# The last stage of a linear-attention and spectral-mixing kernel: the fifth chunks of two batches in one half-wide unit, and more of the adds of x on GpSimd

## The chip, the cores and the metric

One Trainium2 chip; the kernel runs on one of its cores. The metric is the device time in microseconds (us) of one execution. A program's time here is the median of several executions; the profile shows one execution, and its own time stands beside its span below. TensorE is called PE, VectorE DVE, ScalarE ACT, GpSimd POOL and SyncE SP. "SPq" and "ACTq" in the profile are the sequencers of SP and ACT, which issue DMAs.

## The reference

```python
def phi(x):                                   # q, k: (8, 8, 576, 64); w_phi: (64, 128)
    proj = np.einsum('bhsd,df->bhsf', x, w_phi)
    proj = proj - np.max(np.abs(proj), axis=-1, keepdims=True)
    return np.concatenate([np.exp(proj), np.exp(-proj)], axis=-1)
q_p, k_p = phi(q), phi(k)
kv = np.einsum('bhsf,bhsd->bhfd', k_p, v)
z = np.sum(k_p, axis=2)
num = np.einsum('bhsf,bhfd->bhsd', q_p, kv)
den = np.einsum('bhsf,bhf->bhs', q_p, z)[..., None] + 1e-06
x = (num / den).transpose(0, 2, 1, 3).reshape(8, 576, 512)
X = np.fft.rfft(x, axis=1)                    # the first 64 modes are mixed, the others dropped
Yr = einsum('bmd,mde->bme', Xr, w_r) - einsum('bmd,mde->bme', Xi, w_i)
Yi = einsum('bmd,mde->bme', Xr, w_i) + einsum('bmd,mde->bme', Xi, w_r)
y = np.fft.irfft(Y, n=576, axis=1)
u = x + y
out = u + np.maximum(u @ w_ch, 0.0)           # (8, 576, 512) float32
```

## The kernel before

The work has three stages. The first (lines 491 to 583) computes the attention for 32 steps of a batch and two heads (or two batches and one head), and writes x into `xs_all`; the Fourier transform and the first products with `w_r` and `w_i` run in between. The second (lines 661 to 683) waits for the last weights to be loaded, ends the mixing of modes, and computes two products ahead: `xw`, which is x times `w_ch`, and for each batch the spectrum Y (`yall`) and Y times `w_ch` (`zall`), both in bf16. The third (lines 686 to 749) is where the change lies. It computes, for each batch and each chunk of rows,

- relu(x w_ch + irfft(Y w_ch)): in `chan`, PE adds `xw` (through an identity matrix, L689) and `CI` times `zall` (L691) in PSUM, and ACT writes the relu into the output tile (L693);
- x + irfft(Y): in `spec`, PE puts `CI` times `yall` into PSUM (L702), DVE adds it to the output tile (L705), and x is added either by PE, as one more matmul with the identity ahead of L702 (L700), or, in a unit that is called "late", by POOL on the output tile after DVE (L710).

The 576 rows of a batch lie on the partitions in two halves of 288: partition p of the lower half (0 to 63) holds the rows 9p to 9p + 4 as the chunks 0 to 4, and partition 64 + p the rows 9p + 5 to 9p + 8 as the chunks 0 to 3. So the fifth chunk (number 4) of a batch fills the lower 64 partitions alone; its upper half is computed and not used.

A unit of work is two chunks, a PSUM tile of 128 x 2 x 512 floats for each of `chan` and `spec`. There are 20 units, here numbered u0 to u19. For each pair of batches b and b + 4 (b = 0 to 2) there are four wide units (chunks 0 and 1 of batch b, chunks 2 and 3 of it, then the same for batch b + 4), followed by one unit with the fifth chunks of both: u0 to u3 and u4, u5 to u8 and u9, u10 to u13 and u14. The last pair starts with its fifth chunks: u15, and then u16 to u19. Late are, for b up to 2, the first wide unit of each batch and the unit of fifth chunks; in the last pair u15 and u16: 11 of the 20 units.

All of it stands in an order that is written out by hand (`manual_schedule`): each engine takes its instructions in program order. Step n issues `chan` and `spec` of unit n, then on SP the output DMA of the lower half of the partitions, and then on ACT the DMA of the upper half for an earlier unit:

```python
        LAG = 3
        copies.pop(0)()
        for n in range(len(units) + LAG):
            if copies:
                copies.pop(0)()
            if n < len(units):
                u = units[n]
                u["tags"] = ("T2", "T3") if n % 2 == 0 or n < 3 else ("T0", "T1")
                chan(u)
                spec(u)
                for dst, src in u["dmas"][0:1]:
                    nc.sync.dma_start(dst, src)
            for lag, late in ((2, False), (3, True)):
```

An output DMA of a batch carries its chunks 0 to 3 (512 KB for each half of the partitions) and is attached to the second wide unit; in the last pair each wide unit has its own two DMAs of 256 KB. The fifth chunks of two batches leave in one DMA of 256 KB on SP, from the lower half of the partitions (`o4[0:64]`, in the tile `Yacc`). The two PSUM pairs (T2, T3 and T0, T1) alternate: `chan` of unit n waits for the relu of unit n - 2, and `spec` of unit n for DVE's add of unit n - 2. At the start four copies of the last quarter of `zall` (ACT, L656) and `yall` (DVE, L657) stand between the first units.

## Time and profile before

| what | value |
|---|---|
| time of the program | 465.15 us, median of 3 runs (464.51 to 466.84) |
| the profiled execution's own time | 468.21 us |
| its span in the profile | 466.4 us (1.8 us lie around it) |
| the third stage: first matmul of `chan`, last matmul of `spec` | 423.94 us, 456.14 us |
| DVE's last add | 456.75 to 457.97 us |
| first and last issue of an output DMA | 430.48 us, 460.78 us |
| last byte written | about 465.2 us |
| HBM written (the output) | 9.44 MB |

The profile cuts the span into 40 slices of 11.66 us; a digit is an engine's busy share of a slice in tenths, so the third stage is the last four digits of each row. The timeline gives start and duration of each instruction, with the tile that is written, the shapes, and in brackets how long the engine had been idle and who released it. A matmul's row lasts 0.38 us because the array is a pipeline; successive matmuls of 512 columns start 0.216 us apart. "128*64" in a matmul's row means 128 rows and 64 columns of the array in use. q1 is the DMA queue of SP, q10 that of ACT, q0 that of POOL.

### The profile page before, as it was taken

The numbers are of one execution on the slowest core, as the hardware profiler recorded it, in microseconds if no ns is written. First come the engines' busy times: TensorE is split into PE (matmuls) and PEld (weight loads), VectorE is DVE, ScalarE is ACT, GpSimd is POOL, SyncE is SP. The second block draws the span as 40 slices with busy tenths as digits, with TensorE's granted clock in tenths as the row PEclk, the third lists the DMA queues.
The fourth block names the chain that finished last, engine by engine and source line by source line (L and its number), as shares of the span: only waits on it lengthen the run. The fifth ranks groups of instructions, "written<-read, shape, count | busy, mean of one in ns | idle before, by whom it ended". The sixth has DMA issues, their size and how long they took to land.

```text
span 466.4 us, 11013 instructions
## 1 busy us (share of the span) xinstructions
PE 305.9 (66%) x4602; PEld 201.7 (43%) x4615; DVE 301.0 (65%) x414; ACT 254.9 (55%) x516; POOL 199.8 (43%) x253
## 2 busy tenths in 40 slices
PE   2665886735765777657374645566688887867991
PEld 1454664623543645435243433345344444433440
DVE  6688799854988788876455554755322637446882
ACT  3865786743686868765455454555123524516671
POOL 4695477545563346643343333333111221001781
PEclk9997599895899669996777786886799999989997
DMA  8999999999999999999999999999999999930997
GB/s 184 250 249 242 236 216 217 229 206 217 220 228 218 229 218 224 218 229 218 218 214 223 207 229 208 206 207 208 207 207 207 207 207 207 207 65 1 234 317 260
DMA packets 83553, 99.08 MB, mean 212 GB/s; under 512 B 3248, under 2 KB 75568, under 8 KB 82736
## 3 DMA queue, kind: packets, MB, share of 16 engines
q0 software_dynamic: 73872, 74.72, 96.2%
q1 hardware_dynamic: 8672, 19.40, 14.1%
q10 hardware_dynamic: 960, 4.26, 2.9%
q8 instruction: 36, 0.59, 0.5%
q14 instruction: 13, 0.11, 0.1%
HBM read 163.64 MB, written 9.44 MB: 371 GB/s over the span
## 4 chain that ended last, share of the span: by engine, by line
DMA 33%; DVE 21%; issue 20%; PE 13%; ACT 5%; POOL 5%; SPq 1%; DVEq 0%; ACTq 0%; POOLq 0%
DMA wi<-in_moe_w_i_dram 18%; DMA wr<-in_moe_w_r_dram 7%; DVE mkq L222 6%; DMA q<-in_q_dram 4%; DVE xs_all L325 4%; DVE nd L311 3%; DVE tB L304 3%; ACT AA L229 3%; POOL vaug L259 2%; PE psB L689 2%; PE psA L702 2%; PE psB L691 2%; DMA vn<-in_v_dram 2%; DMA qn<-in_q_dram 1%; ACT e L251 1%
## 5 line engine op out<-in xcount | busy, mean ns | idle before, releaser
L259 POOL TENSOR_TENSOR vaug<-vn,ee 128x576 bf16<-128x576 f32 x64 | 72.6, 1152 | 59.6 <-ACT ee L244 50.6
L229 ACT ACTIVATE AA<-psT 128x1024 bf16<-128x1024 f32 x64 | 62.0, 1021 | 47.3 <-PE psT L197 46.8
L151 POOL DMA_DIRECT2D wr<-in_moe_w_r_dram x24 | 21.9, 913 | 113.3 <-PE psY L389 107.6
L251 ACT ACTIVATE e<-mkq 64x4 f32<-64x4 f32 (+1 forms) x128 | 26.3, 206 | 65.8 <-DVE mkq L222 61.4
L233 ACT ACTIVATE AA<-psk 128x1024 bf16<-128x1024 f32 x64 | 61.3, 1009 | 0.0
L624 ACT CAST xw<-psW 128x1024 bf16<-128x1024 f32 x20 | 20.2, 1012 | 54.3 <-PE psW L622 52.3
L389 PE MATMUL psY<-wi,XT 128*32 128x512 bf16 x192 | 25.2, 470 | 34.7 <-DMA wi<-in_moe_w_i_dram 34.7
L389 PEld LDWEIGHTS <-XT 128*32 128x32 bf16 x384 | 18.0, 167 | 64.2 <-issue 53.9
L622 PE MATMUL psW<-wchb,sT 128*128 128x512 bf16 x150 | 38.3, 389 | 3.6 <-ACT xw L624 2.7
L222 DVE TENSOR_REDUCE mkq<-psk 128x8 f32<-128x1024 f32 x32 | 38.8, 1211 | 0.7 <-PE psk L188 0.7
L408 DVE TENSOR_TENSOR Yacc<-psY,Yacc 128x512 f32<-128x512 f32 x16 | 11.0, 689 | 43.5 <-PE psY L389 43.4
L222 DVE TENSOR_REDUCE mkq<-psq 128x8 f32<-128x1024 f32 x32 | 38.9, 1216 | 0.2 <-PE psq L188 0.2
L389 PE MATMUL psY<-wr,XT 128*32 128x512 bf16 x192 | 24.7, 468 | 19.6 <-DMA wr<-in_moe_w_r_dram 8.3
L275 PE MATMUL kvz<-vaug,AA 64*128 64x65 bf16 x1152 | 30.0, 212 | 7.9 <-POOL vaug L264 6.2
L179 DVE COPY kT<-ptr 128x640 bf16<-128x640 bf16 x32 | 15.7, 492 | 29.5 <-PE ptr L173 29.5
L304 DVE TENSOR_TENSOR tB<-psNB,e 128x650 f32<-128x650 f32 x32 | 26.6, 832 | 11.0 <-PE psNB L294 10.3
L294 PEld LDWEIGHTS <-AA 128*128 128x128 bf16 x640 | 29.2, 110 | 10.2 <-issue 8.5
L325 DVE TENSOR_TENSOR xs_all<-nd,rden 128x640 bf16<-128x640 f32 x32 | 31.9, 998 | 1.1
L710 POOL TENSOR_TENSOR of<-of,xs_all 128x1024 f32<-128x1024 f32 x7 | 14.9, 2129 | 38.7 <-DVE of L705 38.5
L275 PEld LDWEIGHTS <-AA 64*128 64x128 bf16 x1152 | 25.7, 108 | 12.1 <-issue 7.9
L197 PE MATMUL psT<-qT,w 64*128 64x512 bf16 x64 | 15.8, 485 | 21.7 <-DVE mkq L222 21.6
L311 DVE TENSOR_TENSOR nd<-psNA,tB 128x650 f32<-128x650 f32 x32 | 26.7, 835 | 3.8 <-DVE tB L304 0.5
(120 smaller groups left out, 713.0 us busy)
## 6 DMA issues: line engine op xcount, KB each, us to landing
wr<-in_moe_w_r_dram POOLq DMA_DIRECT2D x24, 1024.0 KB, 23.8
wi<-in_moe_w_i_dram POOLq DMA_DIRECT2D x24, 1024.0 KB, 28.0
wr<-in_moe_w_r_dram POOLq DMA_DIRECT2D x16, 512.0 KB, 18.6
wi<-in_moe_w_i_dram POOLq DMA_DIRECT2D x16, 512.0 KB, 21.0
vn<-in_v_dram SPq DMA_DIRECT2D x24, 288.0 KB, 5.7
q<-in_q_dram POOLq DMA_DIRECT2D x12, 288.0 KB, 19.9
k<-in_k_dram POOLq DMA_DIRECT2D x12, 288.0 KB, 21.4
out_dram<-of SPq DMA_DIRECT2D x6, 512.0 KB, 6.1
```

What stands on the lines that cost most here:

```text
L222: nc.vector.tensor_reduce(out=o, in_=i, axis=AX.X, op=ALU.max, apply_absolute_value=True)
L229: nc.scalar.activation(AA[:, 0, ab, 0:1024].rearrange("f (x j p) -> f j x p", j=2, p=64), st["psT"].rearrange("f j (x p) -> f j x p", p=64 ...
L233: nc.scalar.activation(AA[:, 1, ab, 0:1024].rearrange("p (c j f) -> p j c f", c=4, j=2), st["psk"], ACT.Exp, scale=sc)
L251: nc.scalar.activation(e2[64 * jj:64 * jj + 64, hh, 0:NCH - jj], mkq[64 * hh:64 * hh + 64, 1, 5 * jj:5 + 4 * jj], ACT.Exp, scale=2.0)
L259: nc.gpsimd.tensor_tensor(out=vaug[:, ab, :, 0:64], in0=st["v"], in1=ee[:, ab, :].unsqueeze(2).to_broadcast([128, 9, D_]), op=ALU.mult,)
L275: nc.tensor.matmul(kvz[:, hh, ab * 65:(ab + 1) * 65], lhsT=AA[r, 1, ab, 128 * j:128 * j + 128], rhs=vaug[r, ab, j, :], start=(j == 0), sto ...
L294: nc.tensor.matmul(p[:, hh, 65 * c:65 * c + 65], lhsT=AA[:, 0, ab, x:x + 128], rhs=kvzF[:, hh, ab * 65:(ab + 1) * 65], start=True, stop=True,)
L304: nc.vector.tensor_tensor(out=tB, in0=st["psNB"], in1=e2.unsqueeze(3).to_broadcast([128, 2, NCH, 65]), op=ALU.mult,)
L311: nc.vector.tensor_tensor(out=nd, in0=st["psNA"], in1=st["tB"], op=ALU.add)
L325: nc.vector.tensor_tensor(out=xo, in0=nd[:, :, :, 0:64], in1=rden.to_broadcast([128, 2, NCH, 64]), op=ALU.mult,)
L389: nc.tensor.matmul(psY[32 * j:32 * j + 32, :], lhsT=XT[:, c0:c0 + 32, m], rhs=wt[ri][:, 2 * j + par, :], start=(par == 0 and ri == 0), sto ...
L622: nc.tensor.matmul(ps[:, x, :], lhsT=sT[:, x, dc, :], rhs=wchb[:, dc, :], start=(dc == 0), stop=(dc == 3))
```

## The change

The fifth chunks of two batches become one chunk: batch b in the partitions 0 to 63, batch b + 4 in 64 to 127. Each of the four units u4, u9, u14, u15 has eight matmuls with 64 columns of weights in place of six with 128, a relu and a DVE add of 512 elements per partition in place of 1024, no POOL add (x comes through PE), and two DMAs of 128 KB, the lower half on SP and the upper on ACT, in place of one of 256 KB. Of the wide units, ten in place of seven are late: for b up to 2 all but the last (u0 to u2, u5 to u7, u10 to u12), and in the last pair u16 as before. So six wide units in place of nine get x through PE. A wide unit's matmuls stand in another order in `spec` (identity for both chunks, then `CI` for both). ACT issues the upper half's DMA of a late unit four steps after it, in place of three; since the DMA of a batch b hangs on its second wide unit, which is late now, it moves from step n + 2 to n + 4, behind that of batch b + 4 in ACT's order (a loop over the lag of 2 comes first). `LAG` is 4.

```diff
+    def parts(u):
+        if "half" not in u:
+            for x, (b, c) in enumerate(u["bc"]):
+                yield slice(0, 128), x, b, c, slice(0, 128)
+        else:
+            for x, (b, c) in enumerate(u["bc"]):
+                yield slice(64 * x, 64 * x + 64), 0, b, c, slice(0, 64)
+
     def chan(u):
         ps = psum.tile([128, 2, DMODEL], F32, name="psB", tag=u["tags"][0])
...
+        todo = list(parts(u))
+        both = [lambda r, x, b, c, m: nc.tensor.matmul(
+                    ps[r, x, :], lhsT=ident_b[:, m], rhs=xw[:, b * NCH + c, :],
+                    start=True, stop=False),
+                lambda r, x, b, c, m: nc.tensor.matmul(
+                    ps[r, x, :], lhsT=CI[:, c, m], rhs=zall[:, b, :], start=False, stop=True)]
+        if "half" in u:
+            for f in both:
+                for a in todo:
+                    f(*a)
+            nc.scalar.activation(u["o"], ps[:, 0, :], ACT.Relu)
...
     def spec(u):
         ps = psum.tile([128, 2, DMODEL], F32, name="psA", tag=u["tags"][1])
...
+        late = u["late"]
+        todo = list(parts(u))
+        if not late:
+            for r, x, b, c, m in todo:
+                nc.tensor.matmul(ps[r, x, :], lhsT=ident_b[:, m], rhs=xs_all[:, b * NCH + c, :],
+                                 start=True, stop=False)
+        for r, x, b, c, m in todo:
+            nc.tensor.matmul(ps[r, x, :], lhsT=CI[:, c, m], rhs=yall[:, b, :],
+                             start=late, stop=True)
+        o = u["o"]
+        nc.vector.tensor_tensor(out=o, in0=ps[:, 0, :] if "half" in u else ps, in1=o, op=ALU.add)
+        if late:
+            b, c = u["bc"][0]
             i = b * NCH + c
...
+            nc.gpsimd.tensor_tensor(out=o, in0=o, in1=xs_all[:, i:i + 2, :], op=ALU.add)
...
-        o4 = Yacc[:, 2 * b:2 * b + 2, :]
+        o4 = Yacc[:, 2 * b, :]
...
-                               late=c == 0 and not (last and x == 1), dmas=dmas))
-        u4 = dict(bc=((b, 4), (b + 4, 4)), o=o4, late=True,
-                  dmas=[(out[b::4].rearrange("x (p n) e -> p x n e", n=9)[:, :, 4, :], o4[0:64])])
+                               late=(x, c) == (0, 0) if last else (x, c) != (1, 2), dmas=dmas))
+        u4 = dict(bc=((b, 4), (b + 4, 4)), o=o4, late=False, half=True,
+                  dmas=[(out[b + 4 * x].rearrange("(p n) e -> p n e", n=9)[:, 4, :],
+                         o4[64 * x:64 * x + 64]) for x in range(2)])
...
-        LAG = 3
+        LAG = 4
...
-            for lag, late in ((2, False), (3, True)):
+            for lag, late in ((2, False), (4, True)):
```

More of the change, by code (lines that the diff above doesn't have):

```diff
@@ L683 @@
         assert not todo and not ahead and len(copies) == 4
+    def parts(u):
[5 more added lines that the diff above has]
+                yield slice(64 * x, 64 * x + 64), 0, b, c, slice(0, 64)
     def chan(u):
         ps = psum.tile([128, 2, DMODEL], F32, name="psB", tag=u["tags"][0])
-        for x, (b, c) in enumerate(u["bc"]):
-            nc.tensor.matmul(ps[:, x, :], lhsT=ident_b, rhs=xw[:, b * NCH + c, :],
-                             start=True, stop=False)
-            nc.tensor.matmul(ps[:, x, :], lhsT=CI[:, c, :], rhs=zall[:, b, :],
-                             start=False, stop=True)
@@ L693, in chan @@
-        nc.scalar.activation(u["o"], ps, ACT.Relu)
+        todo = list(parts(u))
[9 more added lines that the diff above has]
+            nc.scalar.activation(u["o"], ps[:, 0, :], ACT.Relu)
+        else:
+            for a in todo:
+                for f in both:
+                    f(*a)
+            nc.scalar.activation(u["o"], ps, ACT.Relu)
@@ L695, in spec @@
     def spec(u):
         ps = psum.tile([128, 2, DMODEL], F32, name="psA", tag=u["tags"][1])
-        for x, (b, c) in enumerate(u["bc"]):
-            i = b * NCH + c
-            if not u["late"]:
-                nc.tensor.matmul(ps[:, x, :], lhsT=ident_b, rhs=xs_all[:, i, :],
-                                 start=True, stop=False)
-            nc.tensor.matmul(ps[:, x, :], lhsT=CI[:, c, :], rhs=yall[:, b, :],
-                             start=u["late"], stop=True)
-        o = u["o"]
-        nc.vector.tensor_tensor(out=o, in0=ps, in1=o, op=ALU.add)
@@ L706, in spec @@
-        if u["late"]:
-            (b, c), (b1, c1) = u["bc"]
-            i0 = b * NCH + c
-            di = b1 * NCH + c1 - i0
-            nc.gpsimd.tensor_tensor(out=o, in0=o, in1=xs_all[:, i0:i0 + di + 1:di, :], op=ALU.add)
+        late = u["late"]
[4 more added lines that the diff above has]
+                                 start=True, stop=False)
```

## The prediction

> **What bounds the kernel now.** I read the page first: its busy slices say which stage is at a limit.
>
> ```profile
> span 466.4 us, 11013 instructions
> ...
> PE   2665886735765777657374645566688887867991
> ...
> DMA  8999999999999999999999999999999999930997
> GB/s 184 250 249 242 236 216 217 229 206 217 220 228 218 229 218 224 218 229 218 218 214 223 207 229 208 206 207 208 207 207 207 207 207 207 207 65 1 234 317 260
> ```
>
> Nothing ahead of the third stage is changed, so the last four digits count. PE is at 7, 9, 9 and then 1; the DMA row goes 0, 9, 9, 7, at 317 GB/s in the last but one. So from about 431 us PE and the DMAs are both full, and DMAs alone run after PE. The chain of waits says the same: from 430.46 us to 455.7 it is one row of matmuls 0.216 us apart, then ACT 1.03, DVE 1.22, and the outputs.
>
> The groups of 400 to 467 us give the prices.
>
> ```profile
> L705 DVE TENSOR_TENSOR of<-psA,of 128x1024 f32<-128x1024 f32 x16 | 19.6, 1224 | 2.9 <-ACT of L693 2.0
> ...
> L710 POOL TENSOR_TENSOR of<-of,xs_all 128x1024 f32<-128x1024 f32 x7 | 14.9, 2129 | 38.7 <-DVE of L705 38.5
> ...
> L702 PE MATMUL psA<-yall,CI 128*128 128x512 bf16 x39 | 13.1, 379 | 0.6 <-DVE of L705 0.6
> ```
>
> DVE takes 1.22 us a unit and POOL 2.13 (1.26 and 2.18 back to back); the relu (L693) takes 1.02.
>
> The timeline around 440 us shows a queue that costs nothing yet.
>
> ```profile
> 438.13 4.36 POOL L710 TENSOR_TENSOR of<-of,xs_all 128x1024 f32<-128x1024 f32 x2
> ...
> 439.29 1.02 ACT L693 ACTIVATE of<-psB 128x1024 f32<-128x1024 f32 x1 [0.27 <-PE psB L691]
> ...
> 440.29 0.50 ACTq L749 DMA_DIRECT2D out_dram<-of  x1
> ...
> 441.02 1.02 ACT L693 ACTIVATE Yacc<-psB 128x1024 f32<-128x1024 f32 x1 [0.70 <-PE psB L691]
> ...
> 442.31 1.02 ACT L693 ACTIVATE of<-psB 128x1024 f32<-128x1024 f32 x1 [0.27 <-PE psB L691]
> ...
> 442.52 0.50 ACTq L749 DMA_DIRECT2D out_dram<-of  x1
> ```
>
> ACT's DMA for batch 1 stands behind the relu of 439.29 and waits until POOL ends its first add, at 440.29. The next relu, due at 441.02, loses nothing. At 442.5 POOL ends the second add just as the next DMA comes up.
>
> Stretches of the DMA record:
>
> ```profile
> 432.00:434.20 2.20, 2.20 (x12) 1.02 (x11) 2.12 (x2) 1.50 (x2) 1.19 (x1) 1.00 0.90 179
> ...
> 444.00:448.00 4.00, 4.00 (x21) 1.82 (x19) 3.36 (x4) 2.68 (x3) 3.91 (x3) 1.00 1.00 350
> ```
>
> The DMA queues of 432 to 434.2, then of 444 to 448:
>
> ```profile
> q1 hardware_dynamic: 48, 0.39, 90.2%
> ```
>
> ```profile
> q10 hardware_dynamic: 105, 0.71, 52.2%
> q1 hardware_dynamic: 117, 0.69, 48.2%
> ```
>
> With only SP's queue (the lower 64 partitions) moving, it is 179 GB/s at a share of 0.90; with both halves in flight, 350 at 1.00. Both look "busy"; only the second is fast. Over all, 9.44 MB go from the first byte at 431.65 to 465.2: 281 GB/s.
>
> **PE.** Before, u2's `spec` begins at 430.46 and 120 matmuls follow: 120 x 0.2157 = 25.9, so 456.35 (trace: 456.14 + 0.22). After: a late wide unit has 6 slots, another wide one 8, and a half unit 8 matmuls of 64 columns. If two of these run side by side a half unit is 4 slots. From u2's `spec` on: 2 + 8 for u3, 4 half units x 4, u5 to u8 and u10 to u13 26 each, u16 to u19 6 + 3 x 8 = 30: 108 slots, 23.3 us. No row has 64 columns by 512; the bounds are 4 and 8 slots. I take 4, by the nearest: L389's 32-column matmuls.
>
> ```profile
> 396.05 1.24 PE L622 MATMUL psW<-wchb,sT 128*128 128x512 bf16 x5
> 397.22 0.48 PE L389 MATMUL psY<-wr,XT 128*32 128x512 bf16 x4
> ...
> 397.95 0.40 PE L389 MATMUL psY<-wi,XT 128*32 128x512 bf16 x4
> 398.39 0.59 PE L622 MATMUL psW<-wchb,sT 128*128 128x512 bf16 x2
> ```
>
> Four of them go in one slot (397.51, 397.73, 397.95 are 0.22 apart). The rows also price the change of width: L622's last start is 396.91 (396.05 + 4 x 0.2157), L389 starts 0.31 later and not 0.22; on the way back 0.44. That is 0.31 for a pair, in three places (u14 and u15 adjoin): 0.9. So PE alone would end at 430.46 + 23.3 + 0.9 = 454.7, 1.7 earlier.
>
> **DVE and ACT.** A half unit's add is 0.69 (L408, 128x512 from PSUM), the relu between 0.39 (L358, 256 elements) and 1.02; I take 0.56. It saves 4 x 0.53 and 4 x 0.46 on engines that wait for PE anyway: nothing on the path.
>
> **POOL.** Ten adds in place of eleven, but three in a row in each pair of batches: 3 x 2.18 = 6.5 us, against 30 slots = 6.5 of PE. The cover that hid POOL is gone.
>
> **First output.** Batch 0's chunks left SP at 430.48, when DVE ended u1. Now u1 is late: POOL 430.44 to 432.57, so 2.1 later. The DMAs have nothing else to do then: +2.1. On SP the half unit's DMA stands behind batch 4's, which waits for POOL's add of u2 (434.7); DVE ends u4 at about 435, so it loses nothing. No engine waits for SP, but for the reuse of the output tiles: those of pair 0 are gone by 442, and u16 writes them at 451.
>
> **ACT's queue.** From a unit's start, DVE is done 0.65 + 0.42 + 1.02 + 0.05 + 1.23 = 3.37 later (last `chan` matmul, its latency, relu, gap, add), and its relu is due at +1.07. Stepping on:
> - u5 starts 14 slots and a pair of switches after 430.46: 433.8. DVE is done at 437.15; POOL adds until 439.3, 441.5, 443.65 (u5, u6, u7).
> - u10 starts after 44 slots and two pairs of switches: 440.55; its relu goes at 441.6. Behind it stands the DMA of batch 5, which needs POOL's third add: ACT waits until 443.65, then issues two DMAs (0.5 each, the order's new place). Queued behind is u11's relu, due at 442.9: it goes at 444.65, 1.75 late. `chan` of u13 needs that PSUM pair, and `spec` of u13 DVE's add of u11 (446.95, due 445.2).
> - POOL gets u11 at 446.98, ends u12 at 451.25. The relu of u15 is past; the DMA of batch 6 waits for 451.25; u16's relu, due at 450.8, goes at 452.3.
> - u18's `spec` waits for DVE's u16, u19's relu goes at about 456.5, DVE ends at 458.8: 0.8 later than before (457.97), where PE alone had promised 1.7 earlier.
>
> The same steps for before, with its shorter POOL runs, find no late relu and start the last matmul at 456.4 (trace: 456.14). Counting only what was removed would miss this.
>
> **The outputs.** Last data at 458.8 and the 4.4 from issue to landing of before's last DMA (460.78 to 465.2) give 463.2 at least; what is queued decides. Late start: +2.1. Halves: before, SP carried 5.24 MB and ACT 4.19, now 4.72 each; the 1.05 MB that had no partner cost 1.05/184 = 5.7 us alone (184 GB/s: 436.4 to 438.8) and 3.0 at 350, a gain between 0 and 2.7. I take half, -1.4, since the upper half's DMAs of batches 0 and 2 are issued later than the lower half's. A DMA of 128 KB is not in the trace; it gets the issue of the others (0.5) and its bytes, and between half and all of the landing time of the 256 KB ones (3.8 to 4.8 for `Yacc`) is the same within the sums here, as none of them is last. Starvation: batch pair 0 starts at 433.8; 0.5 MB alone to 436.4, 1.84 MB at 350 to 441.7; batch 1's first bytes come 1.15 after 441.5: idle for 1.0, bounds 0 and 1.5, taken 0.7. Sum **+1.4 us**: 466.4 + 1.4 = 467.8 of span, 469.6 with the 1.8 around it. This execution is 3.1 above the median of the runs (468.21 against 465.15), so on the median **466.5 us**. Its own range is 464.5 to 468.0.
>
> **Rivals.**
> 1. *Faster.* If ACT doesn't wait (POOL's third adds in time), PE ends at 454.7, DVE at 456.4, and the DMAs stay two-sided: 9.44 MB at 350 from 433.8 ends at 460.8, but 456.4 + 4.4 = 460.8 too: 4.4 earlier; with half a microsecond of idle DMAs, 461.3 on the median. For it: 350 GB/s is seen for 4 us. Against it: POOL's 6.5 a pair. Chance 0.16.
> 2. *Slower: issues that ACT pays for.* With transfers queued, one issue takes longer:
>
> ```profile
> 449.86 0.97 ACTq L749 DMA_DIRECT2D out_dram<-of  x1
> ...
> 455.76 5.34 ACTq L749 DMA_DIRECT2D out_dram<-of  x4
> ```
>
> 0.97 in place of 0.50 at 449.86; the last four, waits included, stretch over 5.34; SP's longest issue (L745) took 1.54. ACT now issues fourteen (ten before), in clumps of two or three right ahead of relus at u10 to u12 and u15 to u18. If from the third DMA in flight each takes 1.0 to 1.5, four issues add 2.8 to the relus and DVE ends at 461.6. What was queued ahead drains meanwhile, so the end moves by 0 to 2.8; I take three quarters, since the last units hold 2.4 MB: 466.5 + 2.1 = 468.6. It decides once issues between 443 and 455 us pass 0.5. Chance 0.20.
> 3. *The halves never overlap.* ACT's DMA of 432.01 moved nothing until 434.2 (only q1 above). If that holds throughout, the split of the fifth chunks brings nothing: +2.1 + 0.7 = 2.8, 468.0. Chance 0.10: the 350 GB/s speak against. The Trainium skill has this as a rule (SBUF — State Buffer, "Can I just issue two DMAs to hit both halves?"): two DMAs on the two halves of the partitions serialize, with 6% gained. By that rule the sum is 468.0; the trace agrees at 432 us and not at 444 to 448, where 350 is nearly double 179.
> 4. *The half matmuls don't pair.* 16 slots more, 3.45 us, of which the waits and the transfers above hide some two thirds: 467.5. Chance 0.03; L389's rows are against.
>
> **Chances.** Forecast 0.51, rivals 0.16, 0.20, 0.10, 0.03. A measurement here tells 0.5% (2.3 us) from no change: faster than 462.8 is rival 1, 0.16; slower than 467.5 is 2, 3, half of 4 and the forecast's upper edge, 0.34; the rest, 0.50, within. To leave out no more than 2 in 10 the range reaches into 1 and covers 2: 462.0 to 469.2.
>
> **What would show it.** Right: the first output near 432.6; ACTq rows that end at POOL's third add, with a relu late behind them near 444 and 452; PE digits below 9 in the last stage; last matmul past 456. Wrong: POOL done before ACT asks, outputs at 340 GB/s or more from 434 on, or half matmuls 0.2 us apart one by one.

## The result and the profile after

The changed kernel takes 470.33 us, median of 6 runs (469.93 to 471.36); the kernel before, beside it on the same chip, 465.86 (464.51 to 467.69). The ratio is 1.0099, 95% interval 1.0071 to 1.0127: slower by 4.5 us, where the forecast was 466.5 and the range ended at 469.2.

The page of the changed kernel:

```profile
span 468.3 us, 11018 instructions
...
PE   2666876755587777666372746576788887878881
...
DMA  8999999999999999999999999999999999922998
GB/s 186 264 249 236 233 218 226 220 205 229 218 219 225 222 220 219 218 229 218 218 218 218 214 222 207 207 208 208 207 207 207 207 207 207 204 35 45 243 272 248
```

Look at the last four slices. PE no longer reaches 9, so it now waits. The DMA row still says 9, 9, 8, but where before reached 317 GB/s in its fullest slice, none here passes 272. The DMAs are as busy as before and slower. The groups of 400 us to the end show no engine that became slower at its work:

```profile
L730 POOL TENSOR_TENSOR of<-of,xs_all 128x1024 f32<-128x1024 f32 x10 | 21.3, 2129 | 42.2 <-DVE of L726 42.1
L726 DVE TENSOR_TENSOR of<-psA,of 128x1024 f32<-128x1024 f32 x16 | 19.3, 1222 | 12.0 <-ACT of L712 11.7
L712 ACT ACTIVATE of<-psB 128x1024 f32<-128x1024 f32 x16 | 16.0, 1022 | 14.2 <-PE psB L701 6.2 <-DVE of L726 4.1 <-DMA out_dram<-of 2.5
L698 PE MATMUL psB<-xw,ident_b 128*128 128x512 bf16 (+1 forms) x39 | 13.4, 382 | 3.0 <-ACT of L712 2.7
```

Means are as before (2129, 1222, 1022 ns); what grew is idle time: DVE's from 2.9 to 12.0 us. The 2.5 us that the third row puts down to an output DMA are one relu, at 452.34, and not a tile that came free late: the DMAs of its tile had landed by 441.6, and two issues on ACT (450.35 to 452.23) stand right ahead of it.

Spans of single profiles mislead here: the code ahead of the third stage is the same, yet its end differs. The first of the four `zall` copies (L656, ACT), in the trace of before and of after:

```profile
L656 ACT CAST zall<-psZ x4: 999/1002/1005, 423.6 to 428.8; 32x1024 bf16<-32x1024 f32 x4
```

```profile
L656 ACT CAST zall<-psZ x4: 999/1002/1004, 420.8 to 426.1; 32x1024 bf16<-32x1024 f32 x4
```

All kernels of this study start it between 419.7 and 423.7. So every time below that is marked + counts from that copy. From there the last byte of output is written at +41.6 before and +46.1 after: 4.5 us, what the medians say.

ACT's timeline at the first two pairs of batches:

```profile
432.45 1.80 ACTq L770 DMA_DIRECT2D out_dram<-of  x2
434.29 1.02 ACT L712 ACTIVATE of<-psB 128x1024 f32<-128x1024 f32 x1 [1.22 <-PE psA L723]
434.32 2.21 ACTq L770 DMA_DIRECT2D out_dram<-Yacc  x1
436.71 1.94 ACT L712 ACTIVATE of<-psB 128x1024 f32<-128x1024 f32 x2 [1.39 <-DVE of L726]
...
443.46 2.24 ACTq L770 DMA_DIRECT2D out_dram<-Yacc  x1
```

Where an issue took 0.5, three close together (one relu stands between the second and the third) now take 0.53, 1.24 and 2.21, and the relu behind them goes at 436.71, right after the third. That is rival 2, and it was the first suspect.

The DMA record says something else. Before had 350 GB/s at 444 to 448 (+20.4 to +24.4), its two queues at 52% and 48%. After, by windows (length, PE, PEld, DVE, ACT, POOL, then PEclk, DMA share, GB/s): the first 2.2 us of output, and the place of those 4 us:

```profile
431.20:433.40 2.20, 2.20 (x12) 1.02 (x11) 1.20 (x3) 1.07 (x2) 1.21 (x1) 1.00 0.94 197
441.30:445.30 4.00, 3.20 (x15) 1.36 (x14) 2.09 (x2) 1.42 (x2) 2.13 (x1) 1.00 0.99 278
```

A share of 0.99 gives 278, not 350. The queues of after (queue: packets, MB, share of the 16 engines) in 435.9 to 438.9, 441.9 to 444.9, and 444.9 to 447.9:

```profile
q10 hardware_dynamic: 95, 0.66, 83.1%
q1 hardware_dynamic: 74, 0.10, 8.9%
...
q1 hardware_dynamic: 99, 0.68, 91.1%
q10 hardware_dynamic: 12, 0.10, 7.8%
...
q10 hardware_dynamic: 100, 0.68, 72.3%
q1 hardware_dynamic: 100, 0.26, 23.4%
```

The queues take turns: three microseconds of ACT's (upper half), three of SP's (lower half). **Theory of the sides:** while one half of the partitions alone is read, a full set of DMA engines moves some 200 GB/s, and the lag of 4 parts the halves of the first batch of a pair. **Rivals:** the long issues on ACT; the late first output; outputs that end late because they are issued late, whatever they read.

To judge them, four measures from each trace, in us: the last byte; the time from first to last byte; the time of all output packets, divided by the 16 engines that share them; the difference, idle; and for how long one queue was alone (12 or more packets in flight, at most 2 of the other queue; sampled, to about half a microsecond). Each row is read from one profiled execution; the ratios are from all runs.

| kernel | ratio to before, 95% | first byte | last byte | first to last | packets / 16 | idle | one queue alone |
|---|---|---|---|---|---|---|---|
| before | 1 | +8.1 | +41.6 | 33.5 | 31.1 | 2.4 | 14.9 |
| after | 1.0099 [1.0071, 1.0127] | +10.3 | +46.1 | 35.9 | 34.3 | 1.6 | 20.7 |
| e1 | 1.0114 [1.0076, 1.0152] | +10.3 | +46.2 | 36.0 | 34.3 | 1.7 | 21.0 |
| e2 | 0.9977 [0.9955, 0.9998] | +8.1 | +39.8 | 31.7 | 30.5 | 1.2 | 12.7 |
| e3 | 1.0083 [1.0054, 1.0111] | +10.3 | +45.5 | 35.3 | 34.0 | 1.3 | 21.5 |
| e4 | 1.0102 [1.0069, 1.0135] | +10.3 | +46.5 | 36.2 | 32.9 | 3.3 | (one queue) |
| e5 | 1.0071 [1.0048, 1.0094] | +8.1 | +46.3 | 38.2 | 35.8 | 2.4 | 25.8 |
| e6 | 1.0023 [0.9990, 1.0057] | +10.3 | +42.6 | 32.4 | 30.6 | 1.8 | 13.1 |
| e7 | 1.0018 [0.9992, 1.0044] | +8.1 | +42.2 | 34.1 | 31.3 | 2.8 | 14.5 |
| e9 | 1.0108 [1.0077, 1.0140] | +8.1 | +45.6 | 37.5 | 33.7 | 3.8 | 21.5 |
| e10 | 1.0006 [0.9981, 1.0031] | +8.1 | +41.3 | 33.2 | 31.2 | 2.0 | 15.1 |
| e12 | 1.0047 [1.0020, 1.0073] | +8.1 | +44.5 | 36.4 | 32.4 | 4.0 | 16.3 |
| e13 | 1.0058 [1.0035, 1.0081] | +8.1 | +43.9 | 35.8 | 33.6 | 2.2 | 21.1 |
| e14 | 1.0264 [1.0229, 1.0299] | +7.7 | +52.9 | 45.2 | 31.9 | 13.3 | 14.5 |
| e15 | 1.0079 [1.0049, 1.0109] | +10.3 | +45.7 | 35.4 | 33.8 | 1.6 | 21.5 |

After against before: +2.2 late start, +3.2 slower packets, -0.8 idle: the 4.5 us, but for rounding.

### The profile page after: what moved, and what is told of

It is laid out like the page before. It is cut to its first block, busy times and chain, and to the rows that moved or that the text cites. A ratio compares the mean times of both kernels' runs of the same rounds, so it can differ in the third digit from the quotient of the medians.

```text
span 468.3 us, 11018 instructions
## 1 busy us (share of the span) xinstructions
PE 313.4 (67%) x4604; PEld 206.6 (44%) x4617; DVE 298.7 (64%) x414; ACT 253.0 (54%) x516; POOL 199.0 (42%) x252
## 4 chain that ended last, share of the span: by engine, by line
DMA 31%; DVE 22%; issue 20%; PE 9%; POOL 7%; ACT 6%; SPq 1%; ACTq 1%; DVEq 0%; POOLq 0%
DMA wi<-in_moe_w_i_dram 18%; DMA wr<-in_moe_w_r_dram 7%; DVE mkq L222 7%; DMA q<-in_q_dram 4%; DVE xs_all L325 4%; DVE nd L311 3%; DVE tB L304 3%; ACT AA L229 2%; POOL of L730 2%; PE psNB L294 2%; POOL vaug L259 2%; PE ptr L173 2%; DMA kn<-in_k_dram 2%; ACT of L712 1%; SPq L118 1%
## 5 line engine op out<-in xcount | busy, mean ns | idle before, releaser
L730 POOL TENSOR_TENSOR of<-of,xs_all 128x1024 f32<-128x1024 f32 x10 | 21.3, 2129 | 42.2 <-DVE of L726 42.1
L275 PE MATMUL kvz<-vaug,AA 64*128 64x65 bf16 x1152 | 31.6, 218 | 6.7 <-POOL vaug L264 5.2
L294 PEld LDWEIGHTS <-AA 128*128 128x128 bf16 x640 | 31.8, 116 | 8.3 <-issue 6.6
L179 DVE COPY kT<-ptr 128x640 bf16<-128x640 bf16 x32 | 15.7, 491 | 30.9 <-PE ptr L173 30.9
L304 DVE TENSOR_TENSOR tB<-psNB,e 128x650 f32<-128x650 f32 x32 | 26.7, 833 | 10.3 <-PE psNB L294 9.3
L275 PEld LDWEIGHTS <-AA 64*128 64x128 bf16 x1152 | 27.2, 112 | 10.9 <-issue 7.1
L614 DVE COPY sT<-pt 128x1024 bf16<-128x1024 bf16 x20 | 13.8, 691 | 26.0 <-PE pt L611 24.8
L197 PE MATMUL psT<-qT,w 64*128 64x512 bf16 x64 | 15.7, 483 | 21.5 <-DVE mkq L222 21.5
## 6 DMA issues: line engine op xcount, KB each, us to landing
k<-in_k_dram POOLq DMA_DIRECT2D x12, 288.0 KB, 21.1
```

What stands on the lines that cost most here:

```text
L275: nc.tensor.matmul(kvz[:, hh, ab * 65:(ab + 1) * 65], lhsT=AA[r, 1, ab, 128 * j:128 * j + 128], rhs=vaug[r, ab, j, :], start=(j == 0), sto ...
L294: nc.tensor.matmul(p[:, hh, 65 * c:65 * c + 65], lhsT=AA[:, 0, ab, x:x + 128], rhs=kvzF[:, hh, ab * 65:(ab + 1) * 65], start=True, stop=True,)
L304: nc.vector.tensor_tensor(out=tB, in0=st["psNB"], in1=e2.unsqueeze(3).to_broadcast([128, 2, NCH, 65]), op=ALU.mult,)
L730: nc.gpsimd.tensor_tensor(out=o, in0=o, in1=xs_all[:, i:i + 2, :], op=ALU.add)
```

## The experiments

### The parts, and ACT's issues

**e1**, the fifth chunks' second DMA on SP, so that ACT has ten issues again:

```
-                for dst, src in u["dmas"][0:1]:
+                for dst, src in u["dmas"] if "half" in u else u["dmas"][0:1]:
                     nc.sync.dma_start(dst, src)
...
-                    for dst, src in units[n - lag]["dmas"][1:2]:
+                    for dst, src in [] if "half" in units[n - lag] else units[n - lag]["dmas"][1:2]:
```

> The changed kernel, with the four upper-half DMAs of the fifth chunks issued by SP in place of ACT; all else as changed. Three theories of the 4.6 us. Issue theory: ACT's third DMA in a row holds ACT's queue for 2.2 us (1.98 to 2.24 in the changed kernel's trace) and the relus behind it are late; the four go away, 6.6 us of held queue, so 3 to 4.5 us come back: 0.999 to 1.003 of before, and DVE's last add 35 to 36.5 us after the first copy of zall (39.5 in the changed kernel, 34.4 before). POOL theory: three adds in a row on POOL make ACT's DMAs wait and all behind them late, however long an issue is: at most 1 us comes back, 1.008 or more. Transfer theory: the end is set by when the first output starts and how the halves overlap; ACT's queue only has slack: 1.008 to 1.010, with the last byte 45 to 46 us after the first copy of zall (46.1 changed, 41.6 before).

Measured: 471.02 us, 1.0114. ACT's issues fell from 18.4 us in all to 9.6, DVE's last add came 1.7 earlier (+37.8 against +39.5), and the last byte stayed at +46.2.

**e2**, the half units alone: late units and lag as before.

```
-                               late=(x, c) == (0, 0) if last else (x, c) != (1, 2), dmas=dmas))
+                               late=c == 0 and not (last and x == 1), dmas=dmas))
...
-            for lag, late in ((2, False), (4, True)):
+            for lag, late in ((2, False), (3, True)):
```

> One part alone: the fifth chunks in halves, but the wide units' adds of x as before (seven on POOL) and the old lag of 3. Issue theory: the fifth chunks' DMA on ACT still comes close behind two others, but no longer right behind them; 0.5 to 1.5 us of held queue at each of four places, 1.000 to 1.004 of before. POOL theory: without the run of three all of the loss is gone, and 8 matmul slots fewer less 0.9 of switching make it 0.997 to 1.000. Transfer theory: first output as early as before and balanced halves: 0.994 to 0.998.

Measured: 464.38 us, 0.9977. The half units by themselves gain about a microsecond. Its page:

```profile
PE   2576686645686777666565665656688878868992
...
GB/s 178 262 250 245 247 211 220 226 206 219 221 226 217 229 218 221 220 224 223 219 208 226 210 218 218 207 208 209 206 208 207 207 208 207 207 127 1 203 353 263
```

PE is at 9 and 9 again and the outputs reach 353 GB/s in a slice, with the same fourteen issues on ACT as the changed kernel.

**e3**, the other part alone: GpSimd's new share and the lag of 4, the fifth chunks as two full chunks with x through PE and one DMA on SP.

```
+        u4 = dict(bc=((b, 4), (b + 4, 4)), o=o4, late=False,
+                  dmas=[(out[b::4].rearrange("x (p n) e -> p x n e", n=9)[:, :, 4, :], o4[0:64])])
```

> The other part alone: ten of sixteen wide units get x from POOL, with the lag of 4, but the fifth chunks are computed as two full chunks with x through PE, and leave in one DMA on SP as before. Issue theory: ACT has two DMAs in a row and not three; the second takes 1.2 to 1.6, so a small part of the loss is left: 1.001 to 1.005. POOL theory: nearly all of the loss is here: 1.008 to 1.011. Transfer theory: late first output and halves out of balance as before: 1.008 to 1.012.

Measured: 469.40 us, 1.0083. The loss is with this part.

**e4**, every output DMA on SP:

```
-                for dst, src in u["dmas"][0:1]:
+                for dst, src in u["dmas"]:
                     nc.sync.dma_start(dst, src)
...
-                    for dst, src in units[n - lag]["dmas"][1:2]:
+                    for dst, src in []:
```

> The changed kernel with every output DMA issued by SP, none by ACT. Issue theory: ACT pays nothing, and PE and DVE run as the slots say: DVE's last add 34 to 35 us after the first copy of zall; the time is 0.995 to 1.002 unless one queue moves less than two. POOL theory: ACT doesn't wait for POOL either; POOL's own run remains, 0.998 to 1.003. Transfer theory: one queue serves the halves one after the other at 180 to 250 GB/s in place of 281: last byte 47 us or more after the first copy of zall, 1.012 or more, while DVE is done early.

Measured: 470.28 us, 1.0102. DVE ends its last add at 453.48, +32.8, which is 6.7 earlier than in the changed kernel:

```profile
452.25 1.23 DVE L726 TENSOR_TENSOR of<-psA,of 128x1024 f32<-128x1024 f32 x1 [0.45 <-ACT of L712]
```

and the last byte comes at +46.5. A kernel whose arithmetic is done 6.7 us earlier ends no earlier, so the relus behind ACT's issues are not what sets the end there. Alone e4 does not decide, for it has a price of its own: one queue has to move everything, SP spends 31 us on issues, and idle rises to 3.3. With e1, which keeps both queues, it takes the long issues out as the cause. They are real, and hidden.

### The late start, and the lag

**e5**, u1's x through PE again, so that batch 0's chunks leave early (u1 is then no longer late, so ACT's DMA of batch 0 also goes out two steps after u1 and not four):

```
-                               late=(x, c) == (0, 0) if last else (x, c) != (1, 2), dmas=dmas))
+                               late=(x, c) == (0, 0) if last else (x, c) not in ((1, 2),) + (((0, 2),) if b == 0 else ()), dmas=dmas))
```

> The changed kernel, but u1 alone gets x through PE again (two matmuls more), so that the first output doesn't wait for POOL. The issue theory has fallen by now: with ACT's issues gone the time stayed. What is left are the late first output (2.2 us: first issue 9.07 us after the first copy of zall, 6.91 before) and slower transfers (263 GB/s from first to last byte, 281 before). Late-start theory: the first issue is back at 6.9 and the last byte comes 2.0 to 2.4 earlier: 1.004 to 1.006. Side theory (both queues' transfers run one half of the partitions at a time, because the lower half's are issued first and the upper half's later in a clump): the first pair of batches is also better matched, 3 us or more, 1.003 or less. POOL theory (the run of three in each pair): under 1 us, 1.008.

Measured: 470.02 us, 1.0071. The first byte is back at +8.1 and the last one still at +46.3: the 2.2 us given at the start were lost in slower packets (35.8 against 34.3) and idle time (2.4 against 1.6). A late start by itself does not make the loss either. But the theory of the sides, which expected 1.003 or less, missed as well: one queue was alone for longer than in the changed kernel (25.8 us against 20.7). Of the forecasts only that for POOL's run of three adds came near, and e9 shows the loss without such a run.

**e6**, the changed kernel with ACT's DMAs of late units a step earlier:

```
-            for lag, late in ((2, False), (4, True)):
+            for lag, late in ((2, False), (3, True)):
```

> The changed kernel with the lag of late units at 3 in place of 4: the upper half of the first batch of each pair is issued one step earlier, ahead of the second batch's and apart from it, nearer to its lower half on SP. Side theory: the queues alternate less, the rate from first to last byte goes to 275 GB/s or more, 1.5 to 3 us come back, 1.003 to 1.007. Late-start theory: unchanged, 1.009 to 1.011. POOL theory: ACT asks earlier and waits longer for POOL: 1.010 or more.

Measured: 467.77 us, 1.0023. One digit gives back 3.5 of the 4.5 us in the stage. In the second pair the first batch's upper half is now issued beside its lower half (+17.82 on SP, +17.83 on ACT), and the queues share the time. Its record in 447.7 to 450.7 and 453.7 to 456.7:

```profile
q10 hardware_dynamic: 97, 0.54, 54.0%
q1 hardware_dynamic: 92, 0.39, 38.7%
...
q10 hardware_dynamic: 84, 0.50, 53.5%
q1 hardware_dynamic: 80, 0.52, 47.5%
```

DVE's last add comes 3.5 earlier too (+36.0), so e6 by itself does not tell slow packets from late arithmetic. Two things do: in e1 the add came 1.7 earlier and the last byte did not move; and in the changed kernel the DMA engines are idle for only 1.6 of the 35.9 us from first to last byte, less than before, so little of the loss can be time in which they had no data to move.

**e7**, both edits:

> Both of these: u1 through PE and the lag of 3. If late start and sides are two separate causes, the gains add: 0.998 to 1.002, last byte 41 to 42 us after the first copy of zall. If POOL's run of three is what is left, 1.004 or more.

Measured: 467.23 us, 1.0018. Its first byte is 2.2 earlier than e6's and its last one 0.4. Of the 2.4 us that are left against e2, 1.6 are idle time (2.8 against 1.2) and 0.8 slower packets. POOL's three adds hold the second pair's first output until +17.8, where e2 has it at +15.7.

**e9**, the kernel before, with nothing but the place of ACT's DMA of the first batch changed:

```
-                               late=c == 0 and not (last and x == 1), dmas=dmas))
+                               late=c == 0 and not (last and x == 1), dmas=dmas,
+                               lag=4 if c == 2 and x == 0 and not last else None))
...
-            for lag, late in ((2, False), (3, True)):
-                if 0 <= n - lag < len(units) and units[n - lag]["late"] == late:
+            for lag in (2, 3, 4):
+                if 0 <= n - lag < len(units) and (
+                        units[n - lag].get("lag") or (3 if units[n - lag]["late"] else 2)) == lag:
```

> The kernel before with one edit: for the first three pairs, ACT's DMA of the first batch's upper half is put two steps later, into the step of the second batch's upper half, which is where the changed kernel has it; no arithmetic changes, POOL and PE do as before. Theory of the sides: the lower half of the first batch now goes alone and the two upper halves in one lump behind it, so 1.004 to 1.010 (467.9 to 470.7 us), last byte 43.5 to 46 us into the stage against 41.6, and SP's queue and ACT's queue take turns in the DMA's bytes. Rival, late work of POOL: nothing that it does is moved, so 0.998 to 1.002.

Measured: 470.59 us, 1.0108, a loss as large as the changed kernel's, with neither half units nor another add on POOL. It is made up differently: of the 4.0 us to the last byte 2.6 are slower packets and 1.4 idle time, with no late start. ACT's issues are long here too (the second of two took 1.23 to 2.59), and DVE's last add comes 3.1 later (+37.5). The queues take turns as in the changed kernel, here in 434.75 to 437.75 and the 3 us behind it:

```profile
q1 hardware_dynamic: 64, 0.52, 85.9%
...
q10 hardware_dynamic: 104, 0.72, 96.8%
q1 hardware_dynamic: 16, 0.00, 0.3%
```

### Is it the halves, or only that they are late?

**d1**, output DMAs by themselves (`half` issues one DMA of 512 KB, of the half that its last number names; the third stage's computation is left out, so the output is a constant):

```
+        for b in range(8):
+            half(nc.sync, b, 0)
...
+        for b in range(4):
+            half(nc.sync, b, 0)
+            half(nc.sync, b, 1)
...
+        for b in range(4):
+            half(nc.sync, b + 4, 0)
+            half(nc.scalar, b + 4, 1)
```

> The disputed transfers by themselves: the third stage's computation is left out (no chan, no spec; the output is a constant), and output DMAs of 512 KB from 64 partitions are issued in three stretches: eight lower halves on SP; four lower and four upper halves in turn on SP; four lower halves on SP and four upper ones on ACT, at the same time. Side theory: about 218 to 230 GB/s in the first stretch, with packets of 8 KB near 600 ns; 230 to 260 in the second; 330 to 380 in the third, with packets near 310 ns. If the number of transfers in flight sets the rate and not the side: the same rate in all three, 280 or more. If the halves serialize: 200 to 230 in all three.

Its record from 415 to 490 us, 1.9 us a column:

```profile
GB/s 0 0 9 0 0 0 0 70 210 210 210 210 210 210 201 210 201 197 101 70 210 253 350 280 376 328 310 61 140 210 271 345 345 358 345 210 13 134 205 202
```

Lower halves alone: 210. Halves in turn on one queue: 210 at first, then 250 to 376. Halves on two queues: 140 and 210 at first, then 271 to 358.

**d2** crosses what d1 left together: both halves from one queue, one half from two queues.

```
+        for b in range(4):
+            nc.sync.dma_start(rows(b, 0, 128), t)
...
+                nc.sync.dma_start(rows(b, 64 * r, 64 * r + 64), t[0:64])
+                nc.scalar.dma_start(rows(b + 2, 64 * r, 64 * r + 64), t[0:64])
...
+                nc.sync.dma_start(rows(b, 64 * r, 64 * r + 64), t[0:64])
+                nc.scalar.dma_start(rows(b + 2, 64 * r, 64 * r + 64), t[64:128])
```

> Output DMAs by themselves: the third stage's computation is left out, so the output is a constant. Three groups, each behind the end of the one before: four DMAs of 1 MB on SP, each over all 128 partitions; four of 512 KB on SP beside four on ACT, all reading the lower 64 partitions; four of 512 KB on SP from the lower 64 partitions beside four on ACT from the upper 64. If what one half can give is the limit (theory of the sides): over 300 GB/s with packets of 8 KB near 310 to 400 ns in the first group though only one queue works; 195 to 215 GB/s near 620 ns in the second though two queues work; 205 at first and over 300 later in the third. If the number of queues in flight is the limit: some 205 GB/s in the first group, over 300 in the second and the third.

Its windows inside the three groups, the third line being the start of the third group (the last two numbers are DMA share and GB/s):

```profile
432.00:440.00 8.00, 0.00 (x0) 0.00 (x0) 0.00 (x0) 0.00 (x0) 0.00 (x0) 0.50 0.99 411
446.00:460.00 14.00, 0.00 (x0) 0.00 (x0) 0.00 (x0) 0.00 (x0) 0.00 (x0) 0.50 0.99 206
464.00:468.00 4.00, 0.00 (x0) 0.00 (x0) 0.00 (x0) 0.00 (x0) 0.00 (x0) 0.50 0.93 215
468.00:478.00 10.00, 0.00 (x0) 0.00 (x0) 0.00 (x0) 0.00 (x0) 0.00 (x0) 0.50 0.95 320
```

One queue with all 128 partitions: 411 GB/s, a packet of 8 KB in about 315 ns. Two queues on the same 64: 206, a packet in about 630. Two queues on opposite halves: 320, once both move. The share is 0.93 to 0.99 in all of them. So the limit belongs to the half that is read and not to the queue. The Trainium skill has its ground (SBUF — State Buffer, "Door 1: The DMA port swizzle"): partitions 0 to 63 reach 8 of 16 ports, measured there at 196 GB/s for a 1 MiB transfer; 206 agrees.

The packet records of the kernels themselves tie this to the loss. An 8 KB packet that had at most two packets of the other queue beside it took 603 ns at the median before and 600 after; one with five or more beside it took 309 and 313. Neither kind became slower: there are more of the slow kind, 356 of 768 before and 536 after (322 and 131 of the fast kind). The 8 KB packets make 2.7 of the 3.2 us. The table says the same over all runs with two queues: from e2 to e5, 13.1 us more alone go with 5.3 us more of packets, 0.40 for each; from d2's rates one would expect 0.36 to 0.50 (1 - 206/320 and 1 - 206/411).

**e8**, the changed kernel with each DMA over both halves (SP chunks 0 and 1, ACT chunks 2 and 3):

```
+                    if not last:
+                        dmas = []
+                        for k in range(2):
+                            v = out_v[:, 2 * k:2 * k + 2, :]
+                            dst = type(v)(tensor=v.tensor, offset=v.offset,
+                                          ap=[[5 * DMODEL, 2], [9 * DMODEL, 64], [1, 2 * DMODEL]])
+                            dmas.append((dst, of[x][:, 2 * k:2 * k + 2, :]))
```

> The changed kernel with one edit: for the first three pairs, the two output DMAs of a batch no longer split it by halves of the partitions (lower half on SP, upper half on ACT) but by chunks: SP writes chunks 0 and 1 of both halves, ACT chunks 2 and 3 of both. Issue order, queues, number of DMAs, bytes and all arithmetic stay. Theory of the sides (transfers are slow because for microseconds at a stretch only one half of the partitions is being read): the alternation is gone whatever the queues do, so 1.000 to 1.005 of the kernel before (466.5 to 468.5 us), last byte 42 to 44 us into the third stage, over 285 GB/s between first and last byte, against 46.1 and 263. Rival, the theory of late work (what was issued late ends late, whatever it reads, since POOL sets when the outputs are ready): 1.008 to 1.011 as the changed kernel, last byte near 46.

Measured: 562.43 us, 1.2091 [1.2059, 1.2124]. It says nothing on the halves, because such a DMA ran on two engines. From 440 to 520 us, in 40 columns of 2 us:

```profile
DMA  1321112311111111111112211113111111411111
GB/s 53 97 62 53 53 53 71 93 53 51 59 53 53 53 53 53 51 51 53 53 53 84 80 51 51 53 53 111 53 53 53 51 51 53 111 53 53 53 49 53
```

A share of 0.1 at 53 GB/s is 2 engines of 16, and the trace has two packets in flight where the changed kernel has sixteen. The outermost size of its destination is 2. The Trainium skill states this (DMA: Bandwidth & Descriptors, "Why a DMA increments its semaphore by 16 and not by 1"): the number of engines is the largest, up to 16, that divides the slowest dimension of both patterns. The trace agrees.

**e11**, the same split with the half units alone:

> The half-filled chunks as one unit, with the kernel before's share of GpSimd adds and lag of 3, and the output DMAs of the first three pairs split by chunks and not by halves of the partitions, as in the run before with that split. Theory of the sides: what one-sided stretches are left there (about a third of the bytes in slow packets) go too, so 0.990 to 0.996 of the kernel before, last byte 37.5 to 39.5 us into the stage, over 305 GB/s. If the sides don't matter: 0.998 as with the half-filled chunks alone, last byte 39.8.

Measured: 561.58 us, 1.2061 [1.2024, 1.2097], for the same reason; void too.

**e10**, e2 with e1's edit:

> The half-filled chunks as one unit with the kernel before's share of GpSimd adds and its lag of 3, and the fifth chunks' second DMA on SP and not on ACT. Theory of the sides: the two 128 KB DMAs of a pair then run one after the other, a small loss of side by side running against fewer issues on ACT: 0.996 to 1.000, against 0.998 with them on ACT. Theory of ACT's issues (each DMA that ACT issues costs the path what its issue takes): some 2 to 4 us less of issues on ACT, so 0.990 to 0.994.

Measured: 466.04 us, 1.0006. No gain from fewer issues on ACT; packets take 31.2 in place of 30.5.

**e12 and e13**, e9's edit in the second and third pair only; e12 puts the lower half late as well:

```
+                               lag=4 if c == 2 and x == 0 and 0 < b < 3 else None))
...
+                if not u.get("lag"):
+                    for dst, src in u["dmas"][0:1]:
+                        nc.sync.dma_start(dst, src)
+                if n >= 2 and units[n - 2].get("lag"):
+                    for dst, src in units[n - 2]["dmas"][0:1]:
+                        nc.sync.dma_start(dst, src)
```

> The kernel before with one edit, in the second and third pair alone: both output DMAs of the pair's first batch are put behind those of its second batch, the lower half on SP behind SP's, the upper half on ACT behind ACT's, two steps later than before. Both halves stay side by side; 1 MB of output in each of the two pairs is issued some 4 us later. Theory of the sides: only the time in which one half is read alone costs, so 1.000 to 1.004, last byte 41.5 to 43.5 us into the third stage, and less than in the run with the upper half alone put late. Theory of late issue: more bytes are late than in that run, so at least its time, 1.006 to 1.012, last byte 44 to 46.

> The kernel before with one edit, in the second and third pair alone: only ACT's DMA of the first batch's upper half is put two steps later, behind the second batch's; the lower half stays where it was. 0.5 MB in each of the two pairs is issued later. Theory of the sides: lower halves go alone first and the upper ones in a lump, two thirds of what the same edit cost in all three pairs, so 1.005 to 1.009, last byte 43.5 to 45.5. Theory of late issue: half as many bytes are late as in the run with both halves late, so less than its time, 1.002 to 1.006.

Measured: 468.26 us (1.0047) and 468.80 (1.0058); the intervals overlap, so the times decide nothing. The table shows that each paid for something else. Against before's 31.1 and 2.4, e12 has packets of 32.4 and idle of 4.0: its DMAs were late, and the engines ran dry. e13 has 33.6 and 2.2: no more idle time, slower packets. Lateness has a price too, then, and it shows as idle time, of which the changed kernel has less than before (1.6).

**e15**, the changed kernel with the second batch's halves crossed between the queues:

```
+                    if not last and x == 1:
+                        dmas = dmas[::-1]
```

> The changed kernel with one edit: in the first three pairs the second batch's two output DMAs change queues, so that SP writes its upper half and ACT its lower half. Number, size, queue and issue time of every DMA stay; only which half of the partitions each reads is another. The changed kernel's trace shows the 512 KB DMAs starting in the order lower, lower, upper, upper; here it becomes lower, upper, lower, upper. Theory of the sides, in its sharper form (DMAs are served nearly in the order of issue, and two neighbours overlap at full rate only if they read different halves): 1.001 to 1.006, the packets' time summed over the outputs and divided by 16 falls from 34.3 us to 31 to 32.5, last byte 42.5 to 44.5 us into the stage against 46.1. Theory of late issue: nothing is issued earlier, so 1.008 to 1.012 as the changed kernel, last byte near 46.

Measured: 469.33 us, 1.0079. The sharper form of the theory fell: packets 33.8, one queue alone 21.5; time and last byte (+45.7) are close to what late issue forecast, which says nothing on why the packets are slow. In its trace the lower half of batch 0 moves from 432.28 to 434.93, the next DMA on SP, now an upper half, from 434.77 to 437.56, and ACT's, issued at the same moment as that one, starts at 437.38. DMAs issued 2.5 us apart, 2.7 long, follow each other with hardly an overlap, so the order of the halves hardly matters, and being issued at the same moment is not enough. The rate rises only while packets of two opposite halves are in flight at once, as in d2.

**e14**, the changed kernel with each batch in four DMAs of 256 KB:

```
+                    if not last:
+                        dmas = [(out_v[:, 5 * jj + k:5 * jj + k + 2, :],
+                                 of[x][64 * jj:64 * jj + 64, k:k + 2, :])
+                                for k in (0, 2) for jj in range(2)]
...
-                for dst, src in u["dmas"][0:1]:
+                for dst, src in u["dmas"][:len(u["dmas"]) // 2]:
...
-                    for dst, src in units[n - lag]["dmas"][1:2]:
+                    for dst, src in units[n - lag]["dmas"][len(units[n - lag]["dmas"]) // 2:]:
```

> The changed kernel with one edit: in the first three pairs each batch goes out in four DMAs of 256 KB (64 partitions by two chunks) in place of two of 512 KB: SP writes chunks 0 and 1 of the lower and of the upper half where it wrote the whole lower half, ACT chunks 2 and 3 of both where it wrote the whole upper half, at the same places of both queues. Twelve DMAs more to issue. Theory of the sides: neighbours on a queue always read different halves, so 1.000 to 1.006, packets' time over 16 engines 30.5 to 32.5 us against 34.3, in spite of the added issues. Theory of late issue: twelve more issues on two queues that are already late, so 1.012 to 1.020.

Measured: 479.56 us, 1.0264. Packets took 31.9, as the sides expected; the time did not follow. ACT's queue is held by its issues, some of which wait for an earlier output DMA to land (the one of 453.94, in the chain of waits, for SP's of 446.69). The relu behind four of them comes after 4.1 us without work, and idle rose to 13.3:

```profile
434.46 5.06 ACTq L774 DMA_DIRECT2D out_dram<-of  x4
439.56 1.02 ACT L712 ACTIVATE of<-psB 128x1024 f32<-128x1024 f32 x1 [4.09 <-DMA out_dram<-of]
```

## Why the prediction was wrong

**The step that failed** is the term "Halves" of the outputs' sum: "I take half, -1.4", a gain. The packets became slower instead, by 3.2 us. The other two terms of that sum measured +2.2 for +2.1 and -0.8 for +0.7. Point by point:

- *PE and the half units: right.* Two 64-column matmuls go in a slot, 4 slots a unit: a pair starts together (x2 in the rows below) and the next one 0.21 to 0.24 later. The trace of after:

```profile
429.46 0.59 PE L723 MATMUL psA<-yall,CI 128*128 128x512 bf16 x2
429.99 0.41 PE L698 MATMUL psB<-xw,ident_b 128*64 128x512 bf16 x2
430.23 0.38 PE L701 MATMUL psB<-zall,CI 128*64 128x512 bf16 x2
430.44 0.38 PE L720 MATMUL psA<-xs_all,ident_b 128*64 128x512 bf16 x2
430.66 0.38 PE L723 MATMUL psA<-yall,CI 128*64 128x512 bf16 x2
430.97 0.39 PE L698 MATMUL psB<-xw,ident_b 128*128 128x512 bf16 x1
```

  At a change of width the starts are 0.31 apart each way (429.46 + 0.22 to 429.99; 430.66 to 430.97), so a pair of changes costs 0.19 beyond its slots, where 0.31 was taken. DVE's half add took 0.68 (0.69), the half relu 0.60 (0.56). In e4, where no ACT issue is in the way, DVE ends 1.6 us earlier than before: the promised 1.7.
- *First output: right*, +2.16 against +2.1.
- *ACT's queue: right in kind, wrong in size.* Issues were priced at 0.5; the third of a clump took 2.0 to 2.2. DVE's end came 5.1 later, not 0.8. e1 and e4 show that this was covered by the transfers.
- *Starvation: wrong sign.* +0.7 was taken; idle fell by 0.8; slower transfers leave fewer gaps, as I read it.
- *Halves: the failure.* The term counted bytes: SP 5.24 and ACT 4.19 MB became 4.72 each, so 1.05 MB would find a partner. But bytes on two queues are partners only while both are in flight. The lag of 4 puts the upper half of 0.5 MB a whole DMA behind its lower half; one queue was alone for 20.7 us and not 14.9. At 206 GB/s against 320 to 411, those 5.8 us more move 1.2 MB that would take 2.9 to 3.7 us side by side: a loss of 2.1 to 2.9, most of the 3.2. The prediction saw the later issues, and let them halve a gain instead of asking for a loss.

Rival 3 named the mechanism, that halves do not overlap, as all or nothing, and priced it against no gain; the rule of the Trainium skill beside it (SBUF — State Buffer, "Can I just issue two DMAs to hit both halves?", 6%) is too strict for this chip's traces: two queues on opposite halves gave 320 in d2 against 206, once both were moving. For the first 4 us, 464 to 468, they gave 215, hardly more than 206, and there the rule holds. Rival 2's mechanism came, past its point, and did not decide.

**What stays open.** The decisive experiments are e6 and e9 for the place of the DMA, d2 for the halves, and the packet records join the two. No run removed the one-sidedness from the changed kernel with all else equal: e8 and e11 were void, e14 paid elsewhere, and e6 and e9 also moved ACT's issues and the last add. Why two DMAs issued within 10 ns run one after the other at first and mix later was not settled, nor why e5 drew the halves further apart. d1 and d2 are one execution each. The parts do not sum within their medians (e2 -0.2%, e3 +0.8%, together +1.0%), which the intervals allow.

Of all versions, e2, the half units alone, was the fastest, and by its interval faster than both kernels: 0.9977 [0.9955, 0.9998], a gain of some 1.1 us.

## What to carry to other kernels

A DMA share of 0.99 is no rate: read GB/s beside it, and the queues' shares in windows of 3 us. Where outputs leave by halves of the partitions, the two DMAs of a tile must be in flight together; moving one in its queue by a step, for whatever reason, can cost more than the arithmetic saved. Balance by bytes says nothing about balance in time.

## What the runs showed of the hardware that was not expected

- A DMA that ACT issues close behind two others takes 2.0 to 2.2 us to issue, against 0.5 for the first; in the changed kernel's trace these are the ones of `Yacc` (min/median/max ns). It is not their size: in e2, where the same four stand further from the others, they take 0.90 to 1.73, and in e9 the second of two 512 KB DMAs took up to 2.59.

```profile
L770 ACTq DMA_DIRECT2D out_dram<-of x10: 473/1154/1569, 432.4 to 462.4; - x10
L770 ACTq DMA_DIRECT2D out_dram<-Yacc x4: 1977/2216/2237, 434.3 to 454.8; - x4
```

- A destination whose outermost size is 2 puts a 512 KB DMA on 2 of 16 engines: 53 GB/s, and 97 us more in e8.
- Two DMAs issued on two queues 10 ns apart do not start together: ACT's first byte came 3.7 us after its issue (436.18 for 432.45 in after), when SP's was nearly through (436.39).
